# Hidden product of an FNet layer by Strassen's scheme, with its operands prepared beside the sequence product

## The chip, the cores and the metric

The kernel runs on one core of a Trainium2 chip. Its time is device microseconds of one execution, given as the median of several runs. Five engines work side by side, each through its own queue in program order: TensorE (PE, with its weight loads, PEld), VectorE (DVE), ScalarE (ACT), GpSimd (POOL) and SyncE (SP), which only issues DMAs. Queue q1 carries the DMAs that SP issues, q0 those of POOL.

## The reference, cut to what matters

```python
xn = layernorm(x)                            # x: 2048 x 640
a, b = xn @ dft_hid_re.T, xn @ dft_hid_im.T  # 640 x 640 each
s = dft_seq_re @ a - dft_seq_im @ b          # 2048 x 2048 each
g = silu((silu(xn @ w_gate) * (xn @ w_up)) @ w_down)   # 640 x 1536, 1536 x 640
return x + s * g
```

## The kernel before

Products are made in four stages. `seq(k)`, k = 0 to 3, multiplies the sequence matrices (k // 2 picks the row blocks, k % 2 real or imaginary) with the normalized rows and leaves P = C xn in `p_dram`. Then, for j = 0 and 1, come `hid(j)`, which multiplies P with the hidden matrices (the product over columns: 640 real and 640 imaginary rows of the right side) and leaves y in `y_dram`; `gate_up(j)`; and `down(j)`, which multiplies by y, adds x and stores. A call with j handles the 512-row blocks j and j + 2.

Numbers are 32-bit. A factor is split in a high and a low part, each its own operand: ACT writes the high part, DVE the low one (`split`, lines 192, 197, and 199 with a scale). `mm3` (lines 213 to 215) then issues three matmuls of 128 x 128 by 128 x 512 for each block of a product.

The sequence product, gate and up, and down already go by Strassen's scheme with seven products P1 to P7 on two-by-two blocks: rows j and j + 2, two halves of the inner dimension, and column tiles 0 to 1 and 2 to 3; the fifth column tile is multiplied directly (the operands "d1" and "d2"). The helper `strassen` (line 252) does this for down. `hid` (line 786) does not: for either row block it runs ten inner tiles over five column tiles, `product` after `product` into five PSUM banks, splitting ten tiles of the hidden matrices once per call and ten of P per block.

The scheme needs sums. In `seq`, the left sides' sums are made in two ways: by accumulating DMAs of POOL (line 589: loaded data is added to what is in SBUF), and by DVE adds (`add`, line 592). For k over 0, R = C21 is loaded for "d", C22 is accumulated (P5's left side), DVE adds C11 (P6's, line 736), then C12 (P3's, line 742). Y = C11 is loaded for P1, C21 is accumulated onto it after P6's split (line 738), and it is P7's left side.

`xn_t(j)` (line 830) makes the normalized rows for gate and up: it loads rows of x and the vectors of mean and reciprocal deviation, subtracts and multiplies on DVE (line 846), adds (line 860) and splits nine operands, from 56 us ahead of the stage on. `down_operands` (line 508) makes the right sides of down once, beside the first gate and up: each `next(spare)` (lines 960 and 985) makes one of 18 operands and stores it by POOL in `d_dram`; `down` fetches them by SP, 14 and 10 us ahead (line 996).

The order of the work is a written plan. Each step is entered in a `Plan` with a planned time: `prod(lead, ...)` puts it `lead` us before the matmuls that are being planned, `post` behind them, and PE's clock advances 0.226 us per matmul. Then all steps are sorted by planned time and issued, and `place` gives each buffer an address in one of two arenas so that lives don't overlap in the order. So an engine's queue holds its steps in order of planned time. A step whose data is late holds up all that is behind it on its engine; one whose data is early runs early.

## Time and profile before

| what | value |
|---|---|
| median of 3 runs | 992.23 us (991.88 to 992.58) |
| profiled execution | 992.44 us, span 990.3 us |
| granted TensorE clock | 1.000 |
| PE, DVE, ACT, POOL busy | 99%, 72%, 50%, 11% of the span |
| matmuls | 4302 |
| DMA | 180.08 MB, mean 182 GB/s |

A row of the view by stretch gives, for each engine, busy us and instructions, then the granted clock, the mean busy share of the 16 DMA engines, and what they moved. A row of the groups gives line, engine, operation, tiles and shapes, count, then busy us and the mean ns of one, then the idle time of the engine before them with what ended it. A row of the waits reads: who waited for whom, us in total, times, longest.

### The profile page before, as it was taken

The page shows a single profiled execution, that of the slowest core. Times are in us where ns is not written, and L with a number is a line of the kernel's source. Part 1 is how long each engine was busy: PE and PEld are TensorE (multiplying, and loading weights), DVE is VectorE, ACT ScalarE, POOL GpSimd, SP SyncE. Part 2 cuts the span into 40 slices and gives each one's busy share as a digit, 9 for nine tenths or more (in the row PEclk, how much of TensorE's full clock was granted, in tenths as well). Part 3 has the DMA queues.
Part 4 walks back from the last instruction along what each step waited for, and adds up shares of the span by engine and source line. Part 5 has one row for each costly group of instructions (what it writes and reads, how often), then busy time and mean ns, then how long its engine had stood idle before and what let it go on. Part 6 is the DMA issues. An engine that isn't in the chain of part 4 may idle for free. (4 is left out here: it accounts for less than half of the span.)

```text
span 990.3 us, 11726 instructions
## 1 busy us (share of the span) xinstructions
PE 981.1 (99%) x4302; PEld 802.9 (81%) x4302; DVE 710.3 (72%) x927; ACT 497.2 (50%) x712; POOL 105.0 (11%) x175
## 2 busy tenths in 40 slices
PE   8999999999999999999999999999999999999998
PEld 4778888888888888888888888888888888887887
DVE  6999667856785686377678787777577566666686
ACT  5775554655465564434555654444334544445342
POOL 1640201010101010000111110000010100000000
PEclk9999999999999999999999999999999999999999
DMA  9995757675766586832447535679951301106673
GB/s 342 242 226 168 249 136 179 208 210 116 189 219 187 117 236 205 275 135 94 160 149 263 189 139 176 214 258 335 332 177 54 107 28 53 54 27 205 227 266 131
DMA packets 71464, 180.08 MB, mean 182 GB/s; under 512 B 6448, under 2 KB 22064, under 8 KB 71408
## 3 DMA queue, kind: packets, MB, share of 16 engines
q1 hardware_dynamic: 57072, 125.71, 38.0%
q0 software_dynamic: 14336, 53.63, 19.7%
q8 instruction: 33, 0.54, 0.2%
q14 instruction: 23, 0.19, 0.1%
HBM read 145.75 MB, written 33.57 MB: 181 GB/s over the span
## 5 line engine op out<-in xcount | busy, mean ns | idle before, releaser
L213 PE MATMUL ps<-hl 128*128 128x512 f32 x1420 | 551.9, 389 | 1.3 <-ACT raw L979 0.7
L215 PE MATMUL ps<-hl 128*128 128x512 f32 x1420 | 551.5, 388 | 1.1 <-DVE hl L197 1.0
L214 PE MATMUL ps<-hl 128*128 128x512 f32 x1420 | 551.4, 388 | 0.3 <-DVE hl L197 0.3
L192 ACT ACTIVATE hl<-raw 128x1024 fp32r<-128x1024 f32 (+6 forms) x503 | 371.9, 788 | 263.5 <-PE ps L214 63.1
L197 DVE TENSOR_TENSOR hl<-raw,hl 128x1024 fp32r<-128x1024 f32 (+5 forms) x432 | 391.2, 936 | 133.1 <-ACT hl L192 68.3
L213 PEld LDWEIGHTS ps<-hl 128*128 128x128 f32 x1420 | 266.6, 188 | 59.6 <-ACT hl L192 3.2
L215 PEld LDWEIGHTS ps<-hl 128*128 128x128 f32 x1420 | 266.6, 188 | 57.7 <-DVE hl L197 1.8
L214 PEld LDWEIGHTS ps<-hl 128*128 128x128 f32 x1420 | 266.6, 188 | 55.3 <-DVE hl L197 0.8
L241 ACT ACTIVATE raw<-ps 128x512 f32<-128x512 f32 (+1 forms) x122 | 80.3, 676 | 128.9 <-PE ps L215 111.7
L246 DVE TENSOR_TENSOR raw<-ps,raw 128x512 f32<-128x512 f32 (+1 forms) x90 | 71.5, 795 | 58.8 <-PE ps L215 57.7
L980 DVE TENSOR_TENSOR raw<-raw 128x512 f32<-128x512 f32 x24 | 16.6, 692 | 49.3 <-ACT raw L979 49.2
L893 DVE TENSOR_TENSOR raw<-raw 128x256 f32<-128x256 f32 (+1 forms) x96 | 47.7, 518 | 0.0
L199 DVE SCALAR_TENSOR_TENSOR hl<-raw,hl 128x384 fp32r<-128x384 f32 (+5 forms) x71 | 43.0, 605 | 4.9 <-PE ps L214 2.5
L589 POOL DMA_DIRECT2D raw<-in_cs x36 | 31.8, 953 | 132.4 <-DVE raw L592 88.4
L592 DVE TENSOR_TENSOR raw<-raw 128x1024 f32<-128x1024 f32 x28 | 34.1, 1217 | 8.7 <-DMA raw<-in_cs 8.7
L1042 POOL DMA_DIRECT2D out<-raw x10 | 6.7, 672 | 303.1 <-ACT hl L192 187.5
L693 POOL DMA_DIRECT2D p_dram<-raw x24 | 17.2, 758 | 201.8 <-DVE raw L246 151.8
L958 ACT ACTIVATE raw<-raw 128x512 f32<-128x512 f32 x24 | 15.2, 632 | 22.8 <-DVE raw L246 22.8
L846 DVE TENSOR_TENSOR raw<-raw 128x1024 f32<-128x1024 f32 (+1 forms) x24 | 23.9, 1040 | 1.7 <-DMA raw<-in_xt 1.7
L818 POOL DMA_DIRECT2D y_dram<-raw x20 | 10.9, 546 | 132.5 <-ACT raw L241 132.5
L979 ACT ACTIVATE raw<-ps 128x512 f32<-128x512 f32 x24 | 14.3, 595 | 19.2 <-PE ps L215 17.4
L535 POOL DMA_DIRECT2D d_p<-hl x28 | 15.1, 541 | 80.9 <-ACT hl L192 66.9
(48 smaller groups left out, 196.5 us busy)
## 6 DMA issues: line engine op xcount, KB each, us to landing
raw<-in_cs SPq DMA_DIRECT2D x79, 512.0 KB, 6.3
hl<-d_p SPq DMA_DIRECT2D x56, 384.0 KB, 4.3
raw<-in_cs POOLq DMA_DIRECT2D x36, 512.0 KB, 8.4
raw<-in_wb SPq DMA_DIRECT2D x24, 640.0 KB, 3.9
d_p<-hl POOLq DMA_DIRECT2D x28, 384.0 KB, 3.0
raw<-p_dram SPq DMA_DIRECT2D x8, 1280.0 KB, 9.3
p_dram<-raw POOLq DMA_DIRECT2D x16, 512.0 KB, 5.7
raw<-in_hd SPq DMA_DIRECT2D x20, 320.0 KB, 8.4
```

Source lines behind the costliest of these rows:

```text
L192: nc.scalar.activation(like(hl(dst, 0, a, n)), src(), AF.Copy, scale=1.0 if scale is None else scale)
L197: nc.vector.tensor_tensor(lo, src(), hi, op=ALU.subtract)
L199: nc.vector.scalar_tensor_tensor(lo, src(), scale, hi, op0=ALU.mult, op1=ALU.subtract)
L213: nc.tensor.matmul(o, w(0), m(0), start=first, stop=False, skip_group_check=True)
L214: nc.tensor.matmul(o, w(0), m(1), start=False, stop=False, skip_group_check=True)
L215: nc.tensor.matmul(o, w(1), m(0), start=False, stop=True, skip_group_check=True)
L241: pl.post(lambda: nc.scalar.activation(wide(raw(dst, a, n)), pair(b), AF.Copy), pkeys(b), [(dst, a)], after)
L246: pl.post(lambda: nc.vector.tensor_tensor(wide(raw(dst, a, n)), pair(b), wide(raw(other)), op=op), [*pkeys(b), (other, 0)], [(dst, a)], after)
L589: pl.prod(lead, lambda: nc.gpsimd.dma_start(wide(raw(name)), source(q, g), accum_op=ALU.add), [], [(name, 0), (name, 1)], 8)
L592: pl.prod(lead, lambda: nc.vector.tensor_tensor(raw(dst), raw(dst), raw(src), op=ALU.add), [(src, 0)], [(dst, 0)])
L846: pl.prod(46 - 6 * q - 2 * i - half, lambda i=i, op=op, part=part, rows=rows, nb=nb: nc.vector.tensor_tensor(part(), part(), raw(rows, i * ...
L893: pl.prod(lead, lambda o=o, a=a, b=b, op=op: nc.vector.tensor_tensor(o(), a(), b(), op=op), [(w, 0)], [(c, lead)])
```

## The change

`hid` now goes through `strassen` too, with the five inner tiles of a half in groups of 2, 2 and 1 (`HG`). Its left sides are loaded from `p_dram` 20 us ahead and summed on DVE. With `apart`, P6's and P3's sums get buffers of their own. The banks come from an argument `turn` (1 here, j for down as before).

Its right sides (seven operands and two for the fifth column tile, for three groups: 27) are made once, by the former `down_operands` made general, and stored by SP in `h_dram`; `stored` fetches them for both calls, 13, 12 and 11 us ahead. The signs of P2, P3, P4 and d2 are turned in the split.

The left sides of gate and up are no longer made in `xn_t` but by `xn_sums`, in four slices of 128 rows per call and three steps per slice, and stored unsplit in `x_dram`; `xn_t` loads each of nine operands 12 us ahead of its split.

These steps run beside the sequence products 1, 2 and 3: after their runs number 0, 1 and 2 (P1, d, P2) come three, two and four right sides (one group per product), after runs 5, 6, 7 and 8 (P3, P7 and the two of P4) come two, two, one and one steps of row slices. That does all of j = 0 and half of j = 1; the other six steps follow in the first gate and up, one per column tile from the fourth on.

In `seq` with k over 0, DVE's add of C11 for P6 is replaced by an accumulating DMA 7.5 us ahead of P5, and P7's left side is loaded anew (C11 26 us ahead, C21 accumulated 18.5 ahead), where before Y was kept from P1.

Blank lines are left out of this diff.

```diff
     pairs = [(0, 1), (2, 3), (4, 5)]
-    turn = [0]
-    def strassen(tag, groups, get, top, dop, result, end=False):
-        b2, b1, b3 = (pairs[(turn[0] + i) % 3] for i in range(3))
-        turn[0] += 1
+    def strassen(tag, groups, get, top, dop, result, turn, end=False, apart=None):
+        b2, b1, b3 = (pairs[(turn + i) % 3] for i in range(3))
...
-        def accumulate(dst, src, n):
-            (dn, da, dk), (sn, sa, sk) = dst, src
...
+        sum_lead = apart or {"p5": 12, "p6": 12, "p3": 12, "p7": 12}
+        def accumulate(p, dst, src, n, into=None):
+            (dn, da, dk), (sn, sa, sk), (on, oa, ok) = dst, src, into or dst
+            pl.prod(sum_lead[p], lambda: nc.vector.tensor_tensor(raw(on, oa, n), raw(dn, da, n), raw(sn, sa, n), op=ALU.add),
...
+            accumulate("p5", X[g], V[g], n[g], W[g])
             return operand("p5", g, W[g])
         def s_2(g):
-            accumulate(W[g], Y[g], n[g])
+            s1, W[g] = W[g], room("W2", g) if apart else W[g]
+            accumulate("p6", s1, Y[g], n[g], W[g])
             return operand("p6", g, W[g])
         def s_4(g):
-            accumulate(W[g], Z[g], n[g])
+            if apart:
+                W[g], Z[g] = Z[g], W[g]
+            accumulate("p3", W[g], Z[g], n[g])
             return operand("p3", g, W[g])
...
+    HG = (2, 2, 1)
+    d_dram, h_dram = right_side("d", (3, 3)), right_side("h", HG)
...
+    def right_operands(what, store, groups, load, part, key, minus=False):
...
+            for p in ("p1", "p2", "d1", "d2", "p5", "p6", "p4", "p7", "p3") if minus else d_names:
...
+                n = tiles * (256 if p[0] == "p" else P)
+                if minus:
+                    if p == "p5":
+                        own = pl.buf((what, "sum", g), "raw", n)
+                    t = (lambda own=own: raw(own).rearrange("p (f d) -> p f d", d=256)), (own, 0)
+                    made = {"p5": (t, b11, b12, ALU.subtract), "p6": (t, t, b22, ALU.subtract),
+                            "p7": (t, b12, b22, ALU.add), "p4": (t, b21, t, ALU.add)}
...
+                negative = p == "p1" or minus and p in ("p2", "d2", "p3", "p4")
+                split(0, dst, n, a[0], [a[1], key(name, 0), key(name, 1)], scale=-1.0 if negative else None)
...
+                    pl.prod(-4, lambda p=p, g=g, dst=dst, i=i, n=n: (nc.sync if minus else nc.gpsimd).dma_start(
+                        store[p, g][:, i * n:i * n + n], hl(dst, i).bitcast(F32)),
+                        [(dst, "hl"[i], 0)], [(what, "dram", p, g)], 6)
                 yield
...
+    def load_hid(g):
+        n = HG[g]
+        name = pl.buf(("hraw", g), "raw", 2 * n * D)
+        for h in range(2):
+            for k in range(n):
+                pl.prod(6, lambda h=h, k=k: nc.sync.dma_start(
+                    raw(name, (h * n + k) * D, D).rearrange("p (e a) -> p e a", a=P),
+                    hd[h].rearrange("p (e k a) -> p k e a", k=ND, a=P)[:, 2 * g + k]), [], [(name, h)])
...
+    hid_spare = right_operands("Hp", h_dram, HG, load_hid, lambda name, h: raw(name, h * pl.size[name][1] // 2, pl.size[name][1] // 2),
+                               lambda name, *i: (name, *i), True)
+    def stored(what, store, j, leads):
...
+                pl.prod(leads[g], lambda i=i: nc.sync.dma_start(
+                    hl(name, i).bitcast(F32), store[p, g][:, i * n:i * n + n]), [(what, "dram", p, g)], [(name, "hl"[i], 0)])
...
+            if not fresh:
+                for step in ahead[k - 1].get(slot[0], ()):
+                    next(step)
+                slot[0] += 1
...
         def p5(g):
             s = operand("p5", g, R[g])
-            if fresh:
-                accumulate(R[g], 11, g, LEAD["p5", g][1] - 0.1)
+            accumulate(R[g], 11, g, LEAD["p5", g][1] - 0.1 if fresh else 7.5)
             return s
...
         def p6(g):
-            if not fresh:
-                add(R[g], Y[g], 12)
             s = operand("p6", g, R[g])
-            accumulate(Y[g], 21, g, 11.5)
+            if fresh:
+                accumulate(Y[g], 21, g, 11.5)
...
-        run(("p7", lambda g: operand("p7", g, Y[g]), b2, None))
+        def p7(g):
+            if not fresh:
+                Y[g] = load(11, g, 26)
+                accumulate(Y[g], 21, g, 18.5)
+            return operand("p7", g, Y[g])
+        run(("p7", p7, b2, None))
...
     def hid(j):
-        H = {}
-        for half in range(2):
-                    name = pl.buf(("pr", c, ri), "raw", ND * TC)
-                    pl.prod(18, lambda name=name, ri=ri, c=c: nc.sync.dma_start(
-                        wide(raw(name)), p_dram[ri, c].rearrange("k p t -> p k t")), [("pd", ri, c)], [(name, 0)])
-                    h = pl.buf(("hraw", j, i), "raw", D)
-                    pl.prod(18, lambda h=h, ri=ri, d=d: nc.sync.dma_start(
-                        raw(h).rearrange("p (e a) -> p e a", a=P),
-                        hd[ri].rearrange("p (e k a) -> p k e a", k=ND, a=P)[:, d]), [], [(h, 0)])
-                    H[i] = pl.buf(("H", j, i), "hl", 2 * D)
-                    split(8, H[i], D, lambda h=h: raw(h), [(h, 0)], scale=None if ri == 0 else -1.0)
-                ops[i] = pl.buf(("hs", c, i), "hl", 2 * TC)
-                split(8, ops[i], TC, lambda pr=pr, d=d: raw(pr, d * TC, TC), [(pr, 0)])
-            pl.now = start
-            for i in range(2 * ND):
-                product([(b, lambda part, i=i, e=e: hl(H[i], part, e * P, P), lambda part, s=ops[i]: hl(s, part), i == 0)
...
+        def get(q, g):
+            c, ri, n = j + 2 * (q // 10 - 1), q % 10 - 1, HG[g]
+            name = pl.buf(("pr", c, ri, g), "raw", n * TC)
+            pl.prod(20, lambda: nc.sync.dma_start(
+                wide(raw(name)), p_dram[ri, c, 2 * g:2 * g + n].rearrange("k p t -> p k t")), [("pd", ri, c)], [(name, 0)])
+            return name, 0, (name, 0)
...
+        strassen(("hid", j), HG, get, *stored("Hp", h_dram, j, (13, 12, 11)), result, 1,
+                 apart={"p5": 14, "p6": 14, "p3": 13, "p7": 12})
...
+    def xn_sums(j, lead):
+        n = P
+        for s in range(TC // n):
+            name = pl.buf(("xt", j, s), "raw", 2 * ND * n)
+            rows = pl.buf(("rows", j, s), "raw", 4 * n)
+            for h in range(2):
+                c = j + 2 * h
+                for i in range(2):
+                    at = i * S + c * TC + s * n
+                    pl.prod(lead, lambda i=i, h=h, at=at, rows=rows: nc.sync.dma_start(
+                        raw(rows, (2 * h + i) * n, n), mr_dram[at:at + n].unsqueeze(0).to_broadcast([P, n])),
+                        [("mrd", 0)], [(rows, h, i)])
+                pl.prod(lead, lambda c=c, h=h, s=s, name=name: nc.sync.dma_start(
+                    raw(name, h * ND * n, ND * n).rearrange("p (a b) -> p a b", b=n),
+                    xt[c][:, :, s * n:s * n + n].rearrange("k p t -> p k t")), [], [(name, h, q) for q in range(3)])
+            def store(p, s=s, quad=quad, name=name):
+                h, q = x_names[p]
+                pl.prod(-4, lambda: nc.sync.dma_start(
+                    x_dram[j, p].rearrange("p (b t) -> p b t", t=TC)[:, :, s * n:s * n + n], quad(h, q)),
+                    [(name, h, q)], [("xd", j, p, s)], 6)
+            def plus(dst, src, quad=quad, name=name):
+                pl.prod(0, lambda: nc.vector.tensor_tensor(quad(*dst), quad(*dst), quad(*src), op=ALU.add),
+                        [(name, *src)], [(name, *dst)])
+            for h in range(2):
+                for i, op in enumerate((ALU.subtract, ALU.mult)):
+                    part = lambda h=h, name=name: raw(name, h * ND * n, ND * n).rearrange("p (a b) -> p a b", b=n)
+                    pl.prod(0, lambda h=h, i=i, op=op, part=part, rows=rows: nc.vector.tensor_tensor(
+                        part(), part(), raw(rows, (2 * h + i) * n, n).unsqueeze(1).to_broadcast([P, ND, n]), op=op),
+                        [(rows, h, i)], [(name, h, q) for q in range(3)])
+                for p in (("p1", "p2", "d1"), ("p4", "d2"))[h]:
+                    store(p)
+                yield
+            plus((0, 0), (1, 0))
+            plus((1, 0), (1, 1))
+            store("p5")
+            plus((1, 1), (0, 0))
+            store("p6")
+            plus((0, 1), (1, 1))
+            store("p3")
+            store("p7")
+            yield
     def xn_t(j):
-        got = {}
...
-        keep("p1", a[11], 21)
-        plus(a[11], a[21], 18.5)
-        plus(a[21], a[22], 18)
-        keep("p5", a[21], 18)
-        keep("p4", a[22], 16)
...
+        for p, lead in (("p1", 14), ("p5", 12), ("p6", 10.5), ("p2", 9), ("d1", 7.5), ("p3", 6.5), ("d2", 5), ("p7", 4), ("p4", 1)):
+            n = x_dram[j, p].shape[1]
+            name = pl.buf(("xq", j, p), "raw", n)
+            pl.prod(lead + 12, lambda p=p, name=name: nc.sync.dma_start(raw(name), x_dram[j, p][:]),
+                    [("xd", j, p, s) for s in range(4)], [(name, 0)])
+            res[p] = pl.buf(("X", j, p), "hl", 2 * n)
+            split(lead, res[p], n, lambda name=name: raw(name), [(name, 0)])
         return res
...
+    later = xn_sums(1, 6)
...
             if j == 0 and f and f != NF - 1:
                 next(spare, None)
+                if f > 2:
+                    next(later, None)
...
-        strassen(("down", j), [3, 3], get, top, dop, result, j == 1)
+        strassen(("down", j), [3, 3], get, *stored("Tp", d_dram, j, (14, 10)), result, j, j == 1)
+    def ahead_steps():
+        yield from xn_sums(0, 6)
+        for _ in range(6):
+            next(later)
+            yield
+    xs, hs = ahead_steps(), hid_spare
+    when = {0: [hs] * 3, 1: [hs] * 2, 2: [hs] * 4, 5: [xs] * 2, 6: [xs] * 2, 7: [xs], 8: [xs]}
+    ahead.extend([when, when, when])
```

164 lines of the change are left out of this document (64 added, 100 removed).

## The prediction

> **What bounds the kernel now.** I read the page first, then who PE waited for, then the stretches of the span, then the shapes of the groups, and last the DMA view of single stretches. The page and the view of PE's waits:
>
> ```profile
> span 990.3 us, 11726 instructions
> PE 981.1 (99%) x4302; PEld 802.9 (81%) x4302; DVE 710.3 (72%) x927; ACT 497.2 (50%) x712; POOL 105.0 (11%) x175
> ```
> ```profile
> PE ps L463 <- ACT z L1063: 2.3, 1, 2.3
> PE ps L215 <- DVE hl L197: 1.0, 2, 0.5
> PE ps L213 <- ACT raw L979: 0.7, 1, 0.7
> PE ps L213 <- ACT hl L192: 0.5, 1, 0.5
> PE ps L214 <- DVE hl L197: 0.3, 1, 0.3
> PE ps L215 <- DVE hl L199: 0.2, 1, 0.2
> ```
>
> PE is busy for 981.1 of 990.3 us and waits for 5.0 us in all, 2.3 of them at the start. A busy PE row alone would not prove that matmuls are the bound, so the next view is the busy time by stretch (10 to 100 is the first sequence product, the next three lines are the other three, then the first hidden product, the first gate and up, the second hidden product; 8 to 18 and 670 to 690 are stretches in which the DMA engines are full):
>
> ```profile
> core 0: us, PE busy (x) PEld busy (x) DVE busy (x) ACT busy (x) POOL busy (x), PEclk, DMA share, GB/s
> 8.00:18.00 10.00, 10.00 (x34) 5.26 (x32) 6.90 (x21) 6.75 (x13) 0.00 (x0) 1.00 1.03 412
> 10.00:100.00 90.00, 87.95 (x363) 66.98 (x362) 83.29 (x128) 61.80 (x80) 30.08 (x53) 1.00 0.85 244
> 112.00:210.00 98.00, 98.00 (x434) 81.19 (x433) 68.44 (x61) 52.72 (x57) 11.01 (x14) 1.00 0.67 190
> 210.00:308.00 98.00, 98.00 (x434) 81.19 (x433) 68.73 (x61) 52.48 (x57) 11.02 (x14) 1.00 0.64 182
> 308.00:396.00 88.00, 88.00 (x389) 72.88 (x389) 62.76 (x56) 46.22 (x49) 10.49 (x13) 1.00 0.66 178
> 396.00:464.00 68.00, 68.00 (x301) 56.33 (x300) 38.92 (x48) 25.85 (x41) 3.99 (x7) 1.00 0.51 174
> 464.00:610.00 146.00, 145.94 (x643) 120.25 (x642) 116.36 (x217) 82.20 (x166) 22.16 (x41) 1.00 0.49 176
> 684.00:752.00 68.00, 68.00 (x302) 56.31 (x301) 48.09 (x57) 28.08 (x44) 4.73 (x8) 1.00 0.67 223
> 670.00:690.00 20.00, 20.00 (x90) 16.57 (x89) 13.79 (x11) 7.66 (x8) 1.20 (x2) 1.00 1.04 353
> ```
>
> From 112 us on every stretch holds as many matmuls as fit at 98.00 / 434 = 0.2258 us each, the granted clock stays at 1.00, and no other engine ends a wait. So a matmul that isn't issued is worth 0.2258 us in every stage, as long as operands arrive in time. The only stretch with waits in mid-kernel is 10 to 100: there DVE is at 83.29 / 90 = 93% and the DMA engines at 0.85, and PE lacks 2.05 of 90 us. That is the nearest row for what a crowded stage costs. A DMA share of 1.03 or 1.04 means full.
>
> **Matmuls removed.** One call of `hid` multiplies 2 halves x 10 right-hand tiles x 5 column tiles = 100 blocks of three matmuls, 300 in all (the row at 396 shows 301 in 68 us). By the scheme, seven products of 5 x 2 blocks and four of 5 x 1 for the fifth column tile make 90 blocks, 270 matmuls: 61.0 us instead of 67.7. Two calls drop 60 matmuls, 60 x 0.2258 = 13.55 us, all on the path. Everything else in the change is cover, so the rest of the working asks whether three stages still feed PE.
>
> **Sequence products 2 to 4: DVE.** The shapes with their mean ns (ACT makes the high half of a split, DVE the low one):
>
> ```profile
> L192 ACT ACTIVATE hl<-raw 128x1024 fp32r<-128x1024 f32 x191 | 191.6, 1051 | 107.5 <-PE ps L215 30.5 <-PE ps L214 25.9 <-DVE raw L860 14.5
> L197 DVE TENSOR_TENSOR hl<-raw,hl 128x1024 fp32r<-128x1024 f32 x185 | 218.8, 1219 | 68.2 <-ACT hl L192 29.1 <-issue 21.2 <-PE ps L215 10.7
> L197 DVE TENSOR_TENSOR hl<-raw,hl 128x512 fp32r<-128x512 f32 x60 | 41.1, 686 | 26.7 <-issue 8.2 <-ACT hl L192 7.7 <-PE ps L214 6.3
> L592 DVE TENSOR_TENSOR raw<-raw 128x1024 f32<-128x1024 f32 x28 | 34.1, 1217 | 8.7 <-DMA raw<-in_cs 8.7
> L197 DVE TENSOR_TENSOR hl<-raw,hl 128x256 fp32r<-128x256 f32 x77 | 32.2, 418 | 7.4 <-ACT hl L192 7.4
> L246 DVE TENSOR_TENSOR raw<-ps,raw 128x1024 f32<-128x1024 f32 x18 | 22.0, 1223 | 35.2 <-PE ps L215 35.0
> L893 DVE TENSOR_TENSOR raw<-raw 128x640 f32<-128x640 f32 x24 | 19.6, 817 | 0.0
> ```
>
> Each product loses four adds of L592 (4 x 1.217 = 4.9 us). It gains one group of right sides, for two tiles 4 sums and 7 splits of 512 columns (11 x 0.686) and 2 splits of 256 (2 x 0.418): 8.4 us, half of it in the third. And it gains two slices of normalized rows, each 4 x 0.817 + 4 x 0.418 = 4.9 us. 68.6 - 4.9 + 8.4 + 9.9 = 82.0 of 97.5 us (432 matmuls), 84%. That lies between 70%, where PE loses nothing, and 93%, where it loses 2.05 in 90. DVE alone therefore costs little.
>
> **Sequence products 2 to 4: DMA.** The DMA view of the second product, and two full stretches (672 to 700, where most packets are small; 44 to 54, where q0 is nearly all accumulation):
>
> ```profile
> q1 hardware_dynamic: 3214, 11.68, 36.3%
> q0 software_dynamic: 1993, 6.83, 30.7%
> ...
> raw<-in_cs SPq DMA_DIRECT2D x20, 512.0 KB, 5.8
> raw<-in_cs POOLq DMA_DIRECT2D x8, 512.0 KB, 7.3
> ```
> ```profile
> DMA packets 8033, 9.20 MB, mean 328 GB/s; under 512 B 305, under 2 KB 5097, under 8 KB 8032
> ...
> q1 hardware_dynamic: 7664, 7.87, 89.7%
> ```
> ```profile
> q0 software_dynamic: 404, 1.49, 77.8%
> ```
>
> Prices: a plain MB takes 0.363 x 98 / 11.68 = 3.05 us of the sixteen engines, with small packets 0.897 x 28 / 7.87 = 3.19; an accumulated MB takes 0.778 x 10 / 1.49 = 5.22, so one accumulation of 512 KB (0.524 MB) 2.74 us. Each product now has 20 loads and 8 accumulations. Added are 4 loads (11 again for P7) and 4 accumulations (11 onto R, instead of the add), 1.31 MB loaded and 4.19 MB stored for the right sides (half in the last), and twice 1.97 MB for the row slices. The need is 0.67 x 98 = 65.7 now, + 4 x 0.524 x 3.05 = 6.4, + 4 x 2.74 = 11.0, + 9.43 x 3.19 = 30.1: 113 us of 97.5. [...] The lower one takes 412 GB/s for all that isn't accumulated (18.59 - 4.19 + 2.10 + 9.43 = 25.9 MB, 62.9 us) and 12 x 2.74 = 32.9: 96 us. At the 353 GB/s of the other full row it is 106. I take a value next to the lower end: the row at 8 is pure loading, and full engines were reached there without idle gaps. So the engines go from two thirds to nearly full, and this is the risk of the change.
>
> What matters then is the dense part, from P5 to P3 (3 x 48 matmuls, 32.5 us): 8 accumulations, 8 loads, 2.1 MB of right sides, 1.3 MB of results. 21.9 + (4.2 + 2.1 + 1.3) / 0.412 = 40.3 us by the lower prices, 21.9 + 12.8 + 6.7 + 4.0 = 45.4 by the upper. It runs 8 to 13 us behind at its end. Behind it stands P7's left side: load 26 us ahead, accumulation 18.5 ahead, split 10 ahead. A load lands in 5.8 us where it has 7.5, an accumulation is issued in 0.9 (below) and lands in 7.3 where it has 8.5, so the chain has 2.0 to spare, and 10 - 1.05 (ACT) - 1.22 (DVE) = 7.7 us of lead after it. Being 8 late is covered; 12.9 late costs 12.9 - 9.7 = 3.2. SP and POOL are in order, so a store that waits for its split holds the loads behind it, and an early add on DVE that waits for its load holds the splits behind it. I take 1.0 us of waits for the second and third product and 0.5 for the fourth: 2.5, bounds 0 and 9.6.
>
> The accumulations are issued by POOL beside a busy DVE:
>
> ```profile
> L589 POOL DMA_DIRECT2D raw<-in_cs x36: 851/871/1874, 21.6 to 353.4; - x36
> ```
>
> They took 0.87 us to issue, 1.87 at most, with DVE at 70 to 93%. [...]
>
> **Hidden product.** In 61.0 us DVE has 8 left sides of 5 tiles (2 x 1.219 + 0.686 = 3.12 each, 25.0), 4 sums (12.5), 3 combinations (3.7), the splits of gate and up's left sides (7 x 1.219 + 2 x 0.686 = 9.9) the first weights' sums (0.817 + 3 x 0.418 = 2.1) and, by the 0.418 of L197, some 2.4 of their splits: 55.6 us, 91%, where it has 57 to 71% now. The DMA engines carry 5.2 MB of left sides, 10.5 of right sides, 4.2 of row operands, 2.6 of y and 1.3 of weights in about 81 us with the lead: 294 GB/s, under the full rows. Right sides come 11 to 13 us ahead. Bounds: 0, and the crowded stretch's 2.05 / 90 x 122 = 2.8. I take 0.8: the stage is fuller than gate and up (116.36 / 146 = 80%, where PE loses 0.06) and a little less full than the one in which PE loses 2.05.
>
> **Gate and up, first call.** Six column tiles get one step of the second half's row slices, up to 2 x 0.817 on DVE. The fullest columns:
>
> ```profile
> 527.00:539.20 12.20, 12.20 (x55) 9.88 (x54) 10.84 (x21) 6.96 (x14) 1.77 (x4) 1.00 0.69 233
> 539.20:551.40 12.20, 12.20 (x55) 10.13 (x54) 10.84 (x20) 7.05 (x14) 2.54 (x5) 1.00 0.83 299
> ```
> ```profile
> 598.40 0.61 DVE raw L246
> ...
> 599.06 0.50 PE ps L213
> ```
>
> 10.84 + 1.63 = 12.5 of 12.2 us in two columns, and the chain shows that PE started P4 right behind DVE's combination in such a column. Bounds 0 and 2 x 1.63 = 3.3. Recorded durations overlap by a little, and a step that fills a gap of DVE costs nothing, so I take 0.3.
>
> **Sum.** 992.44 (profiled; 990.3 of span) - 13.55 + 2.5 + 0.8 + 0.3 = 982.5. The median of the three runs, 992.23, is 0.2 lower; I leave that out. A difference of 0.2%, 2 us, is about what this kernel's measurement can tell from none.
>
> **Rivals.** (A) The forecast: 0 to 6 us of new waits, 978.4 to 985. For it: zero waits from 112 to 900 us, and leads of 8 us and more. (B) The dense part overtakes the lead in all three products, 3 x 3.2 = 9.6 us, at P7's left side: 992.44 - 13.55 + 9.6 + 1.1 = 989.6, range 985 to 990.7. For it: L592 already lost 8.7 us to late loads. (C) The other side: the DMA engines become the bound of the sequence products. At 353 GB/s the need is 106 us, 8.5 over in the second and third product, about none in the fourth; with 113 it is 15.7, 15.7 and 6.9 over. This gives 992.44 - 13.55 + 1.1 + 17 = 997, and 1018 at worst. It turns the sign from 101.7 us per product on (4.2 over, three times). For it: an accumulation moves only 0.524 / 2.74, 191 GB/s; against it: 412 at the start. [...]
>
> **How the numbers follow.** A 0.62, B 0.18, C 0.20, of which 0.12 ends over 994.4 and 0.07 between. Range: below 978.4 lies nothing but noise, and up to 990 take in A and nearly all of B; C is left out. Faster by over 0.2% is A and nearly all of B (0.79), within 0.2% the mild part of C and B's edge (0.08), slower the rest (0.13).
>
> **What would show it.** 4242 matmuls instead of 4302; each hidden product 61 us; PE busy about 967.5 us; DMA share 0.95 or more in 112 to 396 with DVE near 84%; waits of PE on L192 or L197 only, at P3 and P7 of those products. A span of the second product over 101 us, or adds of DVE that wait for in_cs for tens of us, would prove C; waits in the hidden product over 3 us would prove its term wrong.

## The result, and the profile after

The changed kernel takes 1015.42 us (median of 4, 1013.18 to 1017.17), the kernel before 992.4 (991.88 to 992.8): a ratio of 1.0231, 95% interval 1.0204 to 1.0258. It is slower by 23 us where the prediction had it faster by 10. The profiled execution took 1013.74 us.

The page of the kernel after, its first lines and its DMA line:

```profile
span 1011.9 us, 12333 instructions
...
PE 980.0 (97%) x4242; PEld 795.9 (79%) x4242; DVE 755.5 (75%) x1004; ACT 515.1 (51%) x719; POOL 114.4 (11%) x179
...
DMA packets 123278, 237.69 MB, mean 235 GB/s; under 512 B 11408, under 2 KB 61328, under 8 KB 123216
```

The 60 matmuls are gone (4242), and yet PE is busy for 980.0 us where 967.5 was expected, and it also waits. Who PE waited for, in the kernel after (us in total, times, longest):

```profile
PE ps L213 <- DVE raw L246: 13.9, 6, 4.0
PE ps L214 <- DVE hl L197: 6.6, 6, 2.7
PE ps L469 <- ACT z L1141: 2.3, 1, 2.3
PE ps L213 <- ACT raw L241: 1.5, 2, 0.9
PE ps L213 <- ACT hl L192: 1.2, 2, 0.7
PE ps L215 <- DVE hl L197: 0.8, 2, 0.6
```

The first row is new, and the second stood at 0.3 us before. L246 is DVE's combination of a result, which frees the PSUM banks that P4 needs; L197 is a low part of a split. The stages of the kernel after, bounded by counting matmuls (the stretches of the prediction, at round times, begin 2 to 12 us ahead of their stages): sequence products 2, 3 and 4, first hidden product, first gate and up, second hidden product:

```profile
114.20:218.50 104.30, 100.27 (x434) 82.00 (x433) 80.54 (x86) 57.18 (x65) 14.50 (x18) 0.98 0.95 282
218.50:330.70 112.20, 103.50 (x434) 84.08 (x433) 80.87 (x87) 56.74 (x65) 14.51 (x18) 0.95 0.94 278
330.70:436.70 106.00, 101.39 (x433) 82.51 (x432) 71.58 (x79) 50.61 (x60) 14.60 (x18) 0.97 0.91 269
436.70:498.30 61.60, 61.55 (x271) 50.50 (x270) 46.02 (x52) 32.42 (x40) 3.97 (x6) 1.00 1.02 370
498.35:648.25 149.90, 147.16 (x643) 119.87 (x642) 123.48 (x229) 82.70 (x162) 20.24 (x37) 1.00 0.57 192
723.30:784.50 61.20, 61.20 (x272) 50.69 (x271) 49.22 (x54) 31.23 (x39) 3.97 (x6) 1.00 0.89 318
```

The hidden products take 61.6 and 61.2 us and PE is full, so the gain is there. PE is short in the three sequence products and a little in gate and up. To add this up, take the starts of the matmuls from PE's timeline and sum what lies between neighbours beyond 0.2265 us, where it is clear of rounding (starts over 0.28 us apart). This is the "loss" from here on: waits and slow matmuls together. From 112 to 900 us the kernel before loses 0.5 and the kernel after 34.1:

| kernel after, stretch | loss, us |
|---|---|
| product 2 | 6.2 |
| product 3 | 14.1 |
| product 4 | 7.9 |
| first hidden product | 0.3 |
| first gate and up | 4.4 |
| second gate and up | 1.2 |

992.44 - 13.55 + 33.6 = 1012.5, against 1013.74 measured: the table is the difference but for 1.2 us. The three products lose 28.2, of which the waits are 17.3. By place, the waits are 4.0, 3.9 and 3.9 us in P4 of the three products, behind the combination after P7, then 2.7 us in P6 and 2.0 in P3 of product 3, and 0.7 in all elsewhere. The other 10.9 are matmuls that start late, most of them at half the clock, as three stretches around the longest wait show (kernel after; the first ends with the wait):

```profile
201.40:205.80 4.40, 0.41 (x2) 0.00 (x0) 4.24 (x8) 1.06 (x2) 0.00 (x0) 1.00 1.04 390
205.80:210.00 4.20, 4.16 (x11) 3.29 (x12) 4.17 (x5) 2.90 (x4) 1.30 (x2) 0.59 0.98 316
210.00:214.00 4.00, 4.00 (x19) 3.25 (x19) 3.93 (x7) 1.06 (x1) 0.00 (x0) 1.00 1.07 317
```

PE stands for 4.03 us, and then the granted clock is 0.59 for 4.2 us: 11 matmuls start where 18 or 19 fit. The wait costs 5.9 us, not 4.0. While PE stands, DVE is busy for 4.24 of 4.40 us. What it did before that, from its timeline (start, us, and in brackets what it had waited for):

```profile
185.64 1.68 DVE L936 TENSOR_TENSOR raw<-raw 128x640 f32<-128x640 f32 x2
190.46 1.69 DVE L936 TENSOR_TENSOR raw<-raw 128x640 f32<-128x640 f32 x2 [3.15 <-DMA raw<-in_xt]
192.07 2.35 DVE L197 TENSOR_TENSOR hl<-raw,hl 128x1024 fp32r<-128x1024 f32 x2
194.34 1.22 DVE L246 TENSOR_TENSOR raw<-ps,raw 128x1024 f32<-128x1024 f32 x1
195.47 5.76 DVE L197 TENSOR_TENSOR hl<-raw,hl 128x1024 fp32r<-128x1024 f32 x5
201.15 1.79 DVE L930 TENSOR_TENSOR raw<-raw 128x256 f32<-128x256 f32 x4
202.97 1.68 DVE L936 TENSOR_TENSOR raw<-raw 128x640 f32<-128x640 f32 x2
204.57 1.22 DVE L246 TENSOR_TENSOR raw<-ps,raw 128x1024 f32<-128x1024 f32 x1
```

A slice of rows lands late, DVE stands 3.15 us in front of it with work queued behind, and from then on it runs without a pause up to the combination at 204.57 that P4 waits for: two more steps of slices (L930, L936) lie ahead of it. DVE as a whole is at 75%; what is late is one place in its order. The waits of the queues between 112 and 430 us in the kernel after, from DVE's, ACT's and SP's:

```profile
DVE raw L661 <- DMA raw<-in_cs: 26.0, 7, 6.1
...
DVE raw L936 <- DMA raw<-in_xt: 10.1, 3, 3.8
```
```profile
ACT hl L192 <- DVE raw L661: 37.4, 12, 7.3
ACT hl L192 <- DMA raw<-in_cs: 33.2, 14, 7.4
ACT hl L192 <- DMA raw<-in_hd: 23.9, 4, 11.3
```
```profile
SPq L554 <- ACT hl L192: 44.7, 17, 9.0
SPq L645 <- DMA raw<-in_cs: 39.3, 13, 13.9
...
SPq L554 <- DVE hl L199: 14.2, 6, 7.3
```

L661 is DVE's add in `seq` (L592 before, which waited 8.7 us for in_cs in the whole of the kernel before), L554 a store of a right side, L645 a load of in_cs. I read them as rings: SP stands at a store until ACT has split; ACT stands until the matrix (in_hd) or DVE's add has come; DVE's add stands until a load has landed; and loads of that kind stand behind the store on SP. Stores of the slices (L925) hold SP too, for 33.2 us by their two largest rows. In product 3 the links can be followed one by one, on SP and then on DVE:

```profile
240.38 3.29 SPq L554 DMA_DIRECT2D h_p<-hl  x4
243.78 4.23 SPq L554 DMA_DIRECT2D h_d<-hl  x4
248.11 19.06 SPq L554 DMA_DIRECT2D h_p<-hl  x10
267.22 22.54 SPq L645 DMA_DIRECT2D raw<-in_cs  x9
```
```profile
275.18 1.23 DVE L661 TENSOR_TENSOR raw<-raw 128x1024 f32<-128x1024 f32 x1 [6.06 <-DMA raw<-in_cs]
276.33 2.35 DVE L197 TENSOR_TENSOR hl<-raw,hl 128x1024 fp32r<-128x1024 f32 x2
```

From 240 to 267 us SP issues 18 stores of right sides and no load. An add for P3, which needs one of the loads behind them, stands for 6.06 us; two splits come behind it, and at their end, at 278.74, PE goes on in P6 after its wait of 2.74 us.

The length of a wait on SP alone says little. In the kernel before, which loses nothing, SP stood longer in the same stretch; what differs is ACT, which there waited mostly for PE, with its work done ahead. Two rows of SP's and three of ACT's, kernel before:

```profile
SPq L576 <- DMA p_dram<-raw: 105.6, 9, 24.2
SPq L576 <- DVE hl L197: 82.6, 17, 9.5
```
```profile
ACT raw L241 <- PE ps L215: 41.8, 13, 7.3
ACT hl L192 <- PE ps L214: 40.8, 15, 11.4
ACT hl L192 <- PE ps L215: 40.8, 15, 5.0
```

### The profile page after: what moved, and what is told of

It is laid out like the page before. It is cut to its first block, busy times and chain, and to the rows that moved or that the text cites. A ratio compares the mean times of both kernels' runs of the same rounds, so it can differ in the third digit from the quotient of the medians.

```text
span 1011.9 us, 12333 instructions
## 1 busy us (share of the span) xinstructions
PE 980.0 (97%) x4242; PEld 795.9 (79%) x4242; DVE 755.5 (75%) x1004; ACT 515.1 (51%) x719; POOL 114.4 (11%) x179
## 5 line engine op out<-in xcount | busy, mean ns | idle before, releaser
L213 PE MATMUL ps<-hl 128*128 128x512 f32 x1400 | 548.8, 392 | 17.5 <-DVE raw L246 13.9
L192 ACT ACTIVATE hl<-raw 128x1024 fp32r<-128x1024 f32 (+5 forms) x518 | 391.1, 800 | 319.9 <-DVE raw L979 57.5
L197 DVE TENSOR_TENSOR hl<-raw,hl 128x1024 fp32r<-128x1024 f32 (+5 forms) x442 | 410.2, 963 | 62.0 <-ACT hl L192 41.3
L214 PEld LDWEIGHTS ps<-hl 128*128 128x128 f32 x1400 | 265.0, 189 | 64.5 <-DVE hl L197 10.6
L246 DVE TENSOR_TENSOR raw<-ps,raw 128x512 f32<-128x512 f32 (+1 forms) x96 | 78.9, 822 | 41.8 <-PE ps L215 41.0
L658 POOL DMA_DIRECT2D raw<-in_cs x48 | 42.2, 938 | 177.0 <-DVE hl L197 90.3
L292 DVE TENSOR_TENSOR raw<-raw 128x1024 f32<-128x1024 f32 (+2 forms) x40 | 52.6, 1328 | 12.7 <-DMA raw<-p_dram 12.6
L199 DVE SCALAR_TENSOR_TENSOR hl<-raw,hl 128x256 fp32r<-128x256 f32 (+4 forms) x76 | 43.1, 568 | 20.3 <-ACT hl L192 20.3
L1070 DVE TENSOR_TENSOR raw<-raw 128x512 f32<-128x512 f32 x24 | 16.6, 693 | 47.7 <-ACT raw L1069 47.6
L661 DVE TENSOR_TENSOR raw<-raw 128x1024 f32<-128x1024 f32 x16 | 19.6, 1223 | 26.3 <-DMA raw<-in_cs 26.0
L936 DVE TENSOR_TENSOR raw<-raw 128x640 f32<-128x640 f32 x32 | 26.3, 823 | 10.7 <-DMA raw<-in_xt 10.1
L1046 ACT ACTIVATE raw<-raw 128x512 f32<-128x512 f32 x24 | 15.2, 634 | 23.0 <-DVE raw L246 23.0
L554 POOL DMA_DIRECT2D d_p<-hl x28 | 15.2, 544 | 87.7 <-ACT hl L192 66.4
```

The source lines that it names most:

```text
L192: nc.scalar.activation(like(hl(dst, 0, a, n)), src(), AF.Copy, scale=1.0 if scale is None else scale)
L197: nc.vector.tensor_tensor(lo, src(), hi, op=ALU.subtract)
L199: nc.vector.scalar_tensor_tensor(lo, src(), scale, hi, op0=ALU.mult, op1=ALU.subtract)
L213: nc.tensor.matmul(o, w(0), m(0), start=first, stop=False, skip_group_check=True)
L214: nc.tensor.matmul(o, w(0), m(1), start=False, stop=False, skip_group_check=True)
L246: pl.post(lambda: nc.vector.tensor_tensor(wide(raw(dst, a, n)), pair(b), wide(raw(other)), op=op), [*pkeys(b), (other, 0)], [(dst, a)], after)
```

## The experiments

All ratios are to the kernel before; "products 2 | 3 | 4" is PE's loss in them, 6.2 | 14.1 | 7.9 in the kernel after. The expectations number the theories as they arose: 1 is the amount of DMA, 2 the order of the steps on DVE, 3 and 4 are queues held up by the right sides' stores and loads, 5 is the right sides' work on ACT and DVE, 6 the places in the product where the work stands, 7 both kinds of work together in one product. Line numbers are those of the kernel after. Each run left one profile, so its losses are one execution's: product 2, where the kernel after, the runs with right sides beside product 2 only, with sides not stored and with sides not made all do the same, loses 6.2 to 8.3 in these four. A list that a run writes out two or three times stands here once, under a name.

**Slices later on DVE.** The slices' arithmetic goes 2.5 us behind its place and its stores with it, so that combinations pass it.

```diff
-                pl.prod(-4, lambda: nc.sync.dma_start(
+                pl.prod(-6.5, lambda: nc.sync.dma_start(
...
-                pl.prod(0, lambda: nc.vector.tensor_tensor(quad(*dst), quad(*dst), quad(*src), op=ALU.add),
+                pl.prod(-2.5, lambda: nc.vector.tensor_tensor(quad(*dst), quad(*dst), quad(*src), op=ALU.add),
...
```

> Changed kernel with the arithmetic of the row slices planned 2.5 us later, so that on DVE it stands behind the combination that frees the banks of the next product of the scheme, not in front of it. Nothing is taken away. Theory 1 (full DMA engines make DVE and ACT stand at late loads, and this alone makes PE wait): DVE is as late as before, the three waits for the combination of about 4 us stay at 3 or more, time 1010 to 1016. Theory 2 (the order on DVE: 3.5 us of slices in front of the combination is what turns lateness into a wait): these three waits fall from 4 us to under 1, with them the slow clock behind each (2 us), time 998 to 1003.

1018.77 us, 1.0259 (1.0225 to 1.0294); 3.4 | 16.2 | 9.3. PE's waits in it:

```profile
PE ps L214 <- DVE hl L197: 17.5, 17, 3.4
PE ps L213 <- DVE raw L246: 7.6, 9, 1.6
```

The long waits for combinations are gone (0.6 at most in the three products, as theory 2 had it), and PE waits for splits instead; the time is above both forecasts. The order around the combination decided where PE waits, not how much.

**No slices.** All row slices are left out: gate and up's left sides are loaded from x as it stands, without mean, deviation and sums.

```diff
-    when = {0: [hs] * 3, 1: [hs] * 2, 2: [hs] * 4, 5: [xs] * 2, 6: [xs] * 2, 7: [xs], 8: [xs]}
+    when = {0: [hs] * 3, 1: [hs] * 2, 2: [hs] * 4, }
...
```

> Changed kernel without the row slices: gate and up's left sides are loaded straight from x, not normalized and not summed, so their loads stay and the slices' 4 MB of DMA and 10 us of DVE per product go. Theory 1: DMA share in the second product falls from 0.95 to about 0.83, adds that wait for the sequence matrices fall from 26 us to under 12; time 990 to 996. Theory 2: all three waits for the combination go (18.6 us with the slow clock), the wait at P3 in the third product (8 us) stays; time 992 to 997, adds wait as before.

989.29 us, 0.9951 (0.9936 to 0.9966); 1.1 | 5.5 | 1.9. That is below both forecasts. No wait in P4 is over 0.5 us; two at P3, of 2.9 and 1.4 us, make up most of what stays. The DMA share is 0.88 to 0.91 and not 0.83.

**Right sides beside product 2 only.** Products 3 and 4 get slices and no right sides; the hidden products fetch the first group three times.

```diff
+    less = {i: v for i, v in when.items() if i > 2}
-    ahead.extend([when, when, when])
+    ahead.extend([when, less, less])
...
```

> Changed kernel that makes the hidden product's right sides only for the first group, beside the second sequence product; the third and fourth have none, and the hidden product fetches the first group's data three times. Theory 1: without these 5.5 MB the third product's DMA share falls from 0.94 to about 0.8, its waits at P3 (8 us) go, and since the loads of the slices land in time, the waits for the combination shrink in the third and fourth product; time 998 to 1004. Theory 2: the 8 us at P3 go at most, the three waits of 4 us stay; time 1006 to 1010.

991.81 us, 0.9987 (0.9969 to 1.0006); 7.7 | 0 | 0. Its products 3 and 4:

```profile
219.10:317.00 97.90, 97.90 (x433) 81.07 (x432) 72.50 (x73) 52.24 (x56) 14.56 (x18) 1.00 0.93 257
317.00:415.00 98.00, 98.00 (x434) 81.12 (x434) 68.68 (x67) 48.04 (x51) 14.66 (x18) 1.00 0.96 267
```

Both theories had more, 998 us at least. PE loses nothing at DMA shares of 0.93 and 0.96 and with DVE at 74 and 70%. A high share alone is not what PE waits for: with right sides as well, a share of 0.94 goes with a loss of 14.1. The amount is not the same, though: 91 and 94 us of packet time here, 105 in product 3 of the kernel after, where 97.9 would fit without loss. The run with small accumulations, below, takes that apart.

**P6's and P7's left sides alone.** The kernel before with only that part of the change.

```diff
-            if fresh:
-                accumulate(R[g], 11, g, LEAD["p5", g][1] - 0.1)
+            accumulate(R[g], 11, g, LEAD["p5", g][1] - 0.1 if fresh else 7.5)
...
+                Y[g] = load(11, g, 26)
+                accumulate(Y[g], 21, g, 18.5)
...
```

> Kernel before with only the change in the sequence product: P6's sum by accumulation, P7's left side loaded anew. Four more loads and four more accumulations per product, four adds less. Theory 1: DMA share rises from 0.66 to about 0.83, still no wait of PE; 991 to 993. Rival (the accumulation itself, at half the rate, is the cause of the late loads): adds wait for the sequence matrices for 20 us or more and PE waits 3 us or more per product, 1001 or more.

993.18 us, 1.0004 (0.9993 to 1.0015); 0 | 0 | 0, at DMA shares of 0.82, 0.80 and 0.82, much as theory 1 had it. Four more loads and four more accumulations per product cost nothing by themselves.

**Stores of right sides later.** They are issued 16 us after their place instead of 4, so that SP finds them ready.

```diff
-                    pl.prod(-4, lambda p=p, g=g, dst=dst, i=i, n=n: (nc.sync if minus else nc.gpsimd).dma_start(
+                    pl.prod(-16 if minus else -4, lambda p=p, g=g, dst=dst, i=i, n=n: (nc.sync if minus else nc.gpsimd).dma_start(
```

> Changed kernel with the stores of the hidden product's right sides planned 16 us behind their step, not 4, on the same queue: SP meets them when ACT and DVE have long made the parts. Theory 1 (full DMA engines): bytes and counts are the same, so 1012 to 1017. Theory 3 (SP is in order and stood about 26 us per two products at these stores, so that the loads of the sequence matrices behind them went out up to 12 us late): SP's waits at the stores fall from 70 to under 15 us, adds that wait for the sequence matrices from 26 to under 10 us, time 990 to 998.

1014.29 us, 1.0239 (1.0199 to 1.0278); 10.0 | 15.6 | 0. DVE's waits for in_cs fall from 26.0 to 9.0 us, as theory 3 had it, but ACT's rise from 33.2 to 47.0. The loss moves more than it shrinks (25.6 of 28.2), and the time is that of theory 1.

**Loads of the hidden matrix earlier**, 14 us ahead instead of 6; and **both**, with stores at -12.

```diff
-                pl.prod(6, lambda h=h, k=k: nc.sync.dma_start(
+                pl.prod(14, lambda h=h, k=k: nc.sync.dma_start(
```

> Changed kernel with the loads of the hidden matrices for the right sides 14 us ahead of their step, not 6. Theory 1: 1012 to 1017. Theory 4 (ACT is in order and stood up to 11 us at the first split of a group, since these loads land in 6 to 18 us; what is behind it on ACT, then DVE, is late): ACT's waits for in_hd fall from 24 to under 6 us, the waits of PE fall by about half, 998 to 1005. Theory 3 alone: the stores still hold SP, 1008 to 1015.

> Changed kernel with both: the stores of the right sides 12 us behind their step, the loads of the hidden matrices 14 us ahead. Theory 1: 1012 to 1017. Theories 3 and 4 together: no queue stands any more for the right sides, PE's waits in the second to fourth product under 6 us in all (21 before), 984 to 990, faster than the kernel before.

1018.68 us, 1.027 (1.0246 to 1.0294), 6.2 | 20.5 | 3.8; and 1024.41, 1.0323 (1.0297 to 1.0349), 13.5 | 21.0 | 1.3: slower than any theory had them. In the first ACT no longer waits for in_hd, and its waits for in_cs are 69.2 us. I take it that the loads that went forward passed others that were needed sooner.

**Stores of right sides by POOL** instead of SP.

```diff
-                    pl.prod(-4, lambda p=p, g=g, dst=dst, i=i, n=n: (nc.sync if minus else nc.gpsimd).dma_start(
+                    pl.prod(-4, lambda p=p, g=g, dst=dst, i=i, n=n: nc.gpsimd.dma_start(
```

> Changed kernel with the stores of the right sides issued by POOL, not by SP, at the same planned place. Theory 1: 1012 to 1017. Theory 3: SP's loads are free again, but the accumulations stand behind the stores on POOL instead: P6's and P7's left sides come late; between the changed kernel and the one with later stores, 996 to 1008.

1007.63 us, 1.0143 (1.0118 to 1.0168); 6.5 | 11.2 | 0. The best of the complete kernels that keep the change: 10.5 of 28.2 us come back with SP freed of these stores, and 17.7 stay, within theory 3's range.

**Right sides made, not stored; and moved, not made.** The second and third group are made without their stores; or loaded and stored at the same sizes without ACT's and DVE's work. The hidden products fetch the first group three times in both.

```diff
-                for i in range(2):
+                for i in range(0 if minus and g else 2):
```
```diff
+                if minus and g:
+                    for i in range(2):
+                        pl.prod(-4, lambda p=p, g=g, i=i, n=n, name=name: nc.sync.dma_start(
+                            store[p, g][:, i * n:i * n + n], raw(name, 0, n)), [(name, 0), (name, 1)], [], 6)
+                    yield
+                    continue
...
```

> Changed kernel in which the second and third group of right sides is loaded, summed and split as before beside the third and fourth product, but not stored (4.2 and 2.1 MB of DMA less); the hidden product fetches the first group three times. Theory 1 (the DMA engines are what is full: need of about 97 of 97.5 us per product by recorded share): the third and fourth product lose as little as with no right sides at all, under 2 us together against 25 in the changed kernel; time 990 to 996. Theory 5 (the right sides' work on ACT and DVE, its place in their queues and the wait for its loads): still 15 us or more lost there; 1004 to 1012.

> The counterpart: beside the third and fourth product the hidden matrices are loaded and as many bytes stored from them, unsummed and unsplit, so the DMA of the right sides without their ACT and DVE work. Theory 1: 15 us or more lost in these two products, 1004 to 1012. Theory 5: under 3 us, 990 to 996.

1002.75 us, 1.0093 (1.0061 to 1.0125), 8.3 | 10.6 | 0; and 1005.66, 1.0131 (1.0101 to 1.0161), 7.9 | 7.1 | 1.6. In products 3 and 4, where the two differ from the kernel after, neither half is harmless (10.6 and 8.7), none of both gives 0 (the run with right sides beside product 2 only), and both give 22.0. Theories 1 and 5 each had one of the runs harmless, and neither is.

**One load of C11 for P6 and P7** (DVE adds it for P6, then C21 is accumulated onto it for P7), which takes one accumulation away; and the same with stores by POOL.

```diff
+            if not fresh:
+                Y[g] = load(11, g, 16)
+                add(R[g], Y[g], 10.1)
...
-            if fresh:
-                accumulate(Y[g], 21, g, 11.5)
+            accumulate(Y[g], 21, g, 9.9)
```

> Changed kernel, whole, with one accumulation of four per column group taken out of the sequence product: C11 is loaded once behind P5 (16 us ahead of P6), added by DVE for P6's left side, and kept for P7's, where C21 is accumulated onto it. Per product 11 us of DMA less, 4.9 us of DVE more (89%). Theory 1: need 86 of 97.5 us, DMA share about 0.87, PE's waits in the three products fall from 21 to under 8 us, time 984 to 994. Theory 5 or a limit by DVE: waits stay at 15 us or more, 1006 to 1018.

> The same with the right sides' stores issued by POOL. Theory 1: as before it or a little better, since SP no longer stands at the stores (7.7 us better in the changed kernel), 980 to 990, faster than the kernel before. Limit by DVE: 1002 to 1012.

1017.72 us, 1.0256 (1.0232 to 1.0279), 15.1 | 15.4 | 0 with the DMA share down to 0.82, 0.82 and 0.88; and 1028.6, 1.0364 (1.0333 to 1.0396), 15.3 | 19.2 | 1.3. As a test of the amount they tell little, since they bring a new wait: PE's longest in the first, 6.8 and 8.4 us, fall in P6, behind adds of DVE that stood 8.6 and 7.6 us for a load of in_cs.

**Places swapped.** In products 2 and 3 the slices go behind P1 and d, the right sides behind P7 and P4; and the same with stores by POOL.

```diff
+    swapped = {0: [xs] * 3, 1: [xs] * 3, 6: [hs] * 3, 7: [hs] * 3, 8: [hs] * 3}
-    ahead.extend([when, when, when])
+    ahead.extend([swapped, swapped, when])
```

> Changed kernel, whole, with the two kinds of prepared work in each other's place beside the second and third sequence product: the six steps of row slices behind P1 and d, the nine right sides behind P7 and the two runs of P4 (three each). Bytes, steps and buffers per product are the same; the fourth product is as it was. Theory 1 (amount of DMA): 1010 to 1018. Theory 6 (place: right sides, four of them behind P2, make ACT, DVE and SP late just ahead of P5 to P3, where every step has to be on time): the waits at P3 and in front of P4 in these two products fall from 21.7 us (with the slow clock) to under 8, time 996 to 1004.

> The same with the right sides' stores issued by POOL. Theory 1: 1004 to 1010. Theory 6: 992 to 1000; the fourth product, with the old places, keeps its wait of about 8 us or loses some of it as in the run with stores on POOL.

1023.31 us, 1.0304 (1.0278 to 1.0331), 5.0 | 17.5 | 13.3; and 1025.31, 1.0325 (1.0291 to 1.0358), 7.2 | 16.9 | 15.2. Both are above every forecast. Moving the work to these places doesn't help, POOL as the issuer is no help here either, and the fourth product, whose places didn't change, loses more than before.

**All right sides ahead of P2**, five behind P1 and four behind d.

```diff
-    when = {0: [hs] * 3, 1: [hs] * 2, 2: [hs] * 4, 5: [xs] * 2, 6: [xs] * 2, 7: [xs], 8: [xs]}
+    when = {0: [hs] * 5, 1: [hs] * 4, 5: [xs] * 2, 6: [xs] * 2, 7: [xs], 8: [xs]}
```

> Changed kernel with the four right sides behind P2 moved up to behind P1 and d (five and four steps there), slices where they were. Theory 1: 1010 to 1018. Theory 6: the steps are over about 16 us before P5, so the adds of P3 are on time, their waits for the sequence matrices fall from 26 to under 10 us, the 8 us lost at P3 in the third product go, the waits for the combination behind P7 shrink; 996 to 1006.

1012.24 us, 1.021 (1.0172 to 1.0248); 3.1 | 16.6 | 0, and 5.0 more in the first hidden product: theory 6 is not borne out, since the loss of product 3 stays.

**Small accumulations.** The accumulations of C11 onto R move 64 of 512 columns, in the same number of instructions. This takes 7/8 of four accumulations from each product, 9.6 us of the DMA engines by the prediction's 2.74.

```diff
+        def accumulate(name, q, g, lead, n=TC):
...
+                wide(raw(name))[:, :, :n], source(q, g)[:, :, :n], accum_op=ALU.add), [], [(name, 0), (name, 1)], 8)
```

> Changed kernel in which the accumulations of C11 onto R for P6 (12 in the second to fourth product) move 64 of each tile's 512 columns, so that P6, P3 and what follows from them are not the reference's sums. Count, order, waits and all work of PE, DVE and ACT stay; per product 4 x 2.74 x 7/8 = 9.6 us of the DMA engines go, need 97 to 87 of 97.5. Theory 1 (amount of DMA): PE loses under 8 us in the three products against 29.6 with the slow clock, 988 to 996. Theory 5 (the right sides' and slices' work on ACT and DVE is the larger part): over 18 us lost, 1004 or more. In between: both.

1010.68 us, 1.0176 (1.0148 to 1.0204); 8.1 | 9.4 | 6.3. The share falls to 0.90, 0.88 and 0.86, so that the engines are busy for 96, 95 and 90 us of each product where it was 99, 105 and 96, and 4.4 of 28.2 us come back. All three products now have room for their transfers, and 23.8 us stay lost, as theory 5 had it.

**Rows as before.** A complete kernel: the hidden product by Strassen's scheme with right sides made ahead, but gate and up's left sides made as in the kernel before, 56 us ahead of the stage.

```diff
-    when = {0: [hs] * 3, 1: [hs] * 2, 2: [hs] * 4, 5: [xs] * 2, 6: [xs] * 2, 7: [xs], 8: [xs]}
+    when = {0: [hs] * 3, 1: [hs] * 2, 2: [hs] * 4, }
```

> A whole kernel: the changed one with gate and up's left sides made in SBUF as in the kernel before (56 us ahead, beside the hidden product), so no row slices in the sequence product and no trip through DRAM. The run without slices took 989; the hidden product, where DVE now is at 66%, gets 17 us of DVE work per call. Theory 1: 988 to 994, about the kernel before or a little faster. If DVE is the bound of the hidden product then: 997 or more.

1036.8 us, 1.0448 (1.0426 to 1.0471); 1.5 | 4.6 | 0.9, but the first hidden product:

```profile
414.72:498.99 84.27, 68.34 (x271) 53.56 (x270) 62.14 (x66) 32.05 (x40) 3.96 (x6) 0.92 0.63 223
```

PE lacks 16 of 84 us there; the two hidden products lose 49.7 together. So the row work can't stand beside the shortened hidden product as it stood beside the longer one, and where the change puts it, it costs 28.2 - 7.0 = 21 us in the sequence products. Why it can't is open: DVE is at 74%, and of PE's waits in the whole run 20.7 us are for splits and 10.1 for two fetches of right sides.

**Fewer slices beside the right sides.** A complete kernel: products 2 and 3 carry three steps each instead of six, and the first gate and up all twelve of its half.

```diff
-    ahead.extend([when, when, when])
+    fewer = {0: [hs] * 3, 1: [hs] * 2, 2: [hs] * 4, 6: [xs], 7: [xs], 8: [xs]}
+    ahead.extend([fewer, fewer, when])
...
-                if f > 2:
+                for _ in range(2 if f < 3 else 1):
                     next(later, None)
```

> Whole kernel: beside products 2 and 3 only three steps of row slices each (one behind P7, one behind each run of P4, none behind P3) instead of six; product 4 as in the change; the six steps that this leaves over go to the first gate and up, two per column tile from the second on and one from the fourth. Theory 7 (right sides and slices cost only together in one product, because they share in-order queues, and what they cost grows with both): products 2 to 4 lose between the 8.5 us of no slices and the 28.2 of all of them, some 16, and the first gate and up, where DVE was busy 126 of 149 us, loses 2 to 6 more than in the changed kernel: 1003 to 1010 us. If the slices behind P3 alone were the harm: products 2 and 3 lose as without slices (1.1 and 5.5), 995 to 1000 us. Against both (any slices do it): as the changed kernel, 1013 to 1017.

1017.96 us, 1.0256 (1.0226 to 1.0286); 3.7 | 10.3 | 8.6, and 12.5 in the first gate and up:

```profile
497.57:657.31 159.74, 151.58 (x649) 122.01 (x648) 134.03 (x246) 81.98 (x162) 20.18 (x37) 0.99 0.64 215
```

In products 2 and 3 half the slices give 14.0 us, between the 6.6 of none and the 20.3 of all: the loss grows with their number, and it isn't the slices behind P3 alone. My expected 16 for the three products was too low, since product 4 keeps all its slices (22.6 measured), and gate and up took 8 us more where I had 2 to 6. So theory 7's time was missed: 1017.96 lies beside the 1013 to 1017 that was forecast if slices cost the same in any number, because gate and up lost more than the products gained. No complete kernel among these runs beats the kernel before.

## Why the prediction was wrong

**The matmuls removed: right.** 4242 are left, the hidden products take 61.6 and 61.2 us, and with part of the preparation left out the time comes to 989 to 992, although 8 us are still lost in the products.

**Hidden product, 0.8: right in effect, for a wrong reason.** The loss is 0.3 in the first and 0 in the second. DVE's share there is 46.02 / 61.6 = 75% and 49.22 / 61.2 = 80%, not 91%, so part of the work that the prediction counted doesn't fall in the stage. The DMA share is 1.02 and 0.89 at 370 and 318 GB/s, where the prediction had 294, under the full rows; PE doesn't wait for it.

**Gate and up, 0.3: too small.** 4.4 in the first call, above the bound of 3.3. The first column, which takes no slices, loses 0.9 of it; those that take a step lose 0.3 to 1.2 us each, 3.5 together. DVE is at 123.48 / 149.9 = 82%.

**The need of the DMA engines: near, a little low.** I took a value near 96 us per product. Measured are 0.95 x 104.3 = 99 us in the second and 0.94 x 112.2 = 105 in the third, within the range of 96 (at 412 GB/s) to 113 (by the recorded packet times); that 113 bounds the need from above was my estimate.

**Sequence products, "I take 1.0 us of waits for the second and third product and 0.5 for the fourth: 2.5, bounds 0 and 9.6": the step that failed.** Measured are 28.2 us, three times the upper bound. Of its two reasons, "DVE alone therefore costs little" took DVE's mean share for the measure of a wait. The sum itself held, 82.0 us against 80.54 measured in product 2; but PE waits for one combination or one split, and these were late with DVE idle earlier on, in front of a load. The other reason followed one chain (P7's left side: load, accumulation, splits) through its leads, found 2.0 us to spare, and let that stand for the stage. That chain did hold, as the part tried alone shows (1.0004). PE waited 0.5 us there in the three products, so rival B's place was wrong too. The sign "waits of PE on L192 or L197 only, at P3 and P7" failed with it: 11.9 of the 17.3 us are waits for L246 in P4. The sentence about SP, POOL and DVE being in order was in the prediction and got no term in its sum, and that is what the wait of 2.74 us in product 3 comes from, link by link.

**The clock after a wait** was in no step: with 0.50 for 20.5 us in all between 112 and 430 us (the slow stretches of the last section), it makes up most of the 10.9 of 28.2 us that are no recorded wait.

**Rival C had the sign and the size, 997 to 1018, and not the cause.** Its evidence, adds of DVE that wait for in_cs for tens of us, came true (26.0 us), and so did a second product of over 101 us (104.3). But a share of 0.96 without loss (right sides beside product 2 only), and 23.8 us still lost where the transfers fit in every product (small accumulations, 4.4 us back), show that the amount is a small part. The shares near 0.95 that C and the forecast both expected could not tell them apart.

**What the runs show in its place.** Right sides and slices cost much only together. By their losses in products 2 to 4: neither of them 0, slices alone 0 (in products 3 and 4), right sides alone 8.5 (7.0 with the rows as before), both 28.2. Half of the slices and either half of the right sides (engine work, or transfers) give values in between. By place, waits at P3 come with the right sides and stay without slices (2.9 and 1.4 us); the 4 us in P4 need both, for at most 0.6 us is waited there without slices and nothing without right sides. Every change to a single queue (DVE's order, SP's stores, the loads' lead, the issuer, the place) gave back at most 10.5 us, and waits turned up behind another releaser.

**What stays open.** That the queues interlock, each standing in front of a step that another queue holds up, is how I read the waits of SP, ACT and DVE. One wait of 2.74 us is followed link by link above; for the others, the 4 us in P4 above all, the runs fit it, but none took the order out of the queues, so it is argued and not shown. The slices' loads and stores were never taken off SP, and POOL, which issues both the accumulations and the stores of results, was not looked into: in the kernel after, between 112 and 430 us, its accumulations waited 85.0 us for low parts of splits and 59.3 for loads. How the 28.2 us divide between the queues can't be had by adding up the runs. Whether the change would do better with P7's left side kept from P1 wasn't tried.

## What to carry to other kernels

Work put under cover is judged by what it does to the order of in-order queues: list for each stage everything that is added to the same queues, and test the parts together, because here two parts that cost 0 and 8.5 us alone cost 28.2 together. A mean busy share of an engine or of the DMA engines, 77% and 0.95 in product 2 here, says neither that there is room nor that there is none; the wait that ends last does, and it can be read only once the steps stand in their order. Before moving work off a stage that shrinks, compare what it costs in the new place with the gain of 13.55 us, at its bad end, and give that end a real chance when three queues get new work at once.
